# Gate weights in a pool of their own, their rows reused for the experts' outputs, and the last gate on VectorE alone

## The chip, the core and the metric

The kernel runs on one core of one Trainium2 chip. The metric is the device time of one execution in microseconds (us), as the median of several runs. Engines are called PE (TensorE, matrix products), DVE (VectorE), ACT (ScalarE), POOL (GpSimd) and SP (SyncE, which here only issues DMAs). "L794" is line 794 of the kernel before; in the changed kernel the numbers of the same lines are four or five less (L794 is L790 there, L815 is L811), and just above the edit one more (L505 is L506).

## What is computed

Three layers follow each other. Attention through a packed set of 32 queries per head gives a 512-wide row per token (4608 tokens). A dense layer pair with squared relu follows, and then a top-1 mixture of 8 experts:

```python
x = attn_out.transpose(0, 2, 1, 3).reshape(B * S, H * D)   # 4608 x 512
h = np.maximum(x @ w_in, 0.0)                              # 4608 x 2048
x = h * h @ w_out                                          # 4608 x 512
logits = x @ w_gate + modality_bias[modality_id]           # 4608 x 8
e_idx = np.argmax(logits, axis=1)
probs = softmax(logits); gate_w = probs[np.arange(N), e_idx]
for e in range(E):
    mask = e_idx == e
    h = np.maximum(x[mask] @ w1[e], 0.0)                   # 1024 wide
    out[mask] = gate_w[mask, None] * (h @ w2[e])
```

## The kernel before, in words

The dense pair works through the tokens in 12 units of 384 tokens (`NUN`, three tiles of 128 each, `UT`). For each of 16 pieces f of the hidden width, `layer1` makes `ph` in PSUM, relu and square on ACT, and splits the result into a rounded part and a remainder (`ghl`), so that three products of full-speed matmuls make one accurate product; `layer2` adds them into three banks `acc` (L492). At the end of a unit `evacuate` copies the three banks to the tile `row` in SBUF (two by ACT, L505; one by DVE, L503), and `tail` computes the gate: for each of the 3 token tiles and 8 experts one DVE instruction (L515) multiplies `row` by that expert's row of `wgb` and sums it into one logit. `wgb` holds the gate weights, copied to every partition: 8 rows of 512 numbers, 16 KB a partition. Then follow the bias, the softmax, a store of the rows to DRAM (`x2_d`), and `route`, which sorts the tokens into groups of 512 of one expert.

For every unit but the last the gate runs beside the next unit's matmuls. The last unit has nothing of the dense pair behind it. There the gate is shared out in the kernel before: experts 0 to 4 stay on DVE, and for experts 5 to 7 POOL makes the product into one tile `prod` (L519) and ACT sums it (L520): three tiles by three experts, nine pairs, which all use the one tile `prod`.

Behind that the experts start. `group(g)` takes 512 tokens of one expert: for each of eight pieces f it makes `h` in PSUM (L784), ACT writes the relu into the tile `ht` (L794), DVE writes its remainder (L795), and the second product (L806) adds into the banks `o`; DVE multiplies by the gate's probability (L815), and POOL scatters the row to `out` by an indirect DMA (L817). Weights come by DMAs that SP issues (`wraw`), and are split by ACT (L720) and DVE (L721) into `head`, `ring` and `wbt`. The first `h` of group 0 is already made while the last unit's second layer is running, since its tokens and weights are there.

SBUF room is handed on from stage to stage. `wgb` and `pp32` lie in the pool `pp`; with the pools `at` and `g` (which holds `ghl`, `r` and `prod`) it belongs to the stack `st3`. `st3` is closed behind the last gate, and the pools `o` (eight tiles for the experts' outputs, 16 KB a partition) and `h` (eight tiles `ht`) are opened over the same room:

```python
    other = [tail(NUN - 1), route(NTL - UT, NTL)]
    pull(other, 100)
    st3.close()
    held["o"] = ctx.enter_context(tc.tile_pool(name="o", bufs=8, side="left"))
    held["h"] = ctx.enter_context(tc.tile_pool(name="h", bufs=NFE, side="left"))
    tables(G_A, G_MAX)
    for g in range(G_ALL):
        with tc.high_priority(offset=200 if g == 0 else 0):
            group(g, g + 1 < G_ALL)
```

The order on each engine is made by a scheduler from the order of the code, priorities, and what waits for what. An instruction that writes the first tile of a pool waits for the last readers of the pools whose room it takes. Engines carry out their instructions in order.

Of the kernel before, what the change touches and what calls it, by code (L numbers as in the profile page):

```python
# [10 lines left out]
F32 = mybir.dt.float32  # L11
# [4 lines left out]
AF = mybir.ActivationFunctionType  # L16
ALU = mybir.AluOpType
# [3 lines left out]
P = 128  # L21
# [5 lines left out]
def tile_pack_attention_moe_moe2(  # L27
# [15 lines left out]
    nc = tc.nc  # L43
    B, H, D, S = kT_d.shape
    NPK = pT_d.shape[1] * 2 // (B * H)
    NT, DM = out.shape
    DFF = w_in64.shape[1]
    NE, _, FE = w1.shape
# [11 lines left out]
    NUN = NT // UW  # L60
# [5 lines left out]
    NTT = GT // P  # L66
# [15 lines left out]
    held = {"early": ps0.enter_context(tc.tile_pool(name="ps0", bufs=2, space=PSUM))}  # L82
    st1 = ExitStack()
    st2 = ExitStack()
    st3 = ExitStack()
    w_p = ctx.enter_context(tc.tile_pool(name="raw", bufs=2, side="left"))
    pp_p = st3.enter_context(tc.tile_pool(name="pp", bufs=1, side="left"))
    pw_p = st1.enter_context(tc.tile_pool(name="pw", bufs=1, side="right"))
    a_p = st2.enter_context(tc.tile_pool(name="a1", bufs=2, side="right"))
    
    ident = const.tile([P, P], F32, name="ident")
    make_identity(nc, ident)
    wgb = pp_p.tile([P, NE, DM], F32, name="wgb")
    pp32 = pp_p.tile([P, B, HP, 2 * NPK], F32, name="pp32")
    nc.gpsimd.memset(pp32, 0.0)
    pphl = pw_p.tile([P, PAIRS, 2, HP, 2 * P // 2], F32R, name="pphl")
# [38 lines left out]
    row = rows[:, : UT * XR].rearrange("p (t x) -> p t x", t=UT)  # L135
    junk = rows[:, UT * XR : UT * XR + DM]
# [118 lines left out]
    def bank(tag, name):  # L255
        if "early" in held:
            return held["early"].tile([P, 512], F32, tag="e", name=name, bufs=4)
        return held["all"].tile([P, 512], F32, tag=tag, name=name, bufs={"acc": 3, "h": 2, "t": 3}[tag])
# [128 lines left out]
    def second(f):  # L387
        return blocks(2 * f, 2).rearrange("p k x c f -> p (k x c f)").rearrange("p (x f) -> p x f", x=2)
# [118 lines left out]
    def tail(u):  # L507
        js = slice(u * UT, (u + 1) * UT)
        lg = lg_all[:, js, :]
        prod = held["g"].tile([P, DM], F32, tag="ghl", name="prod") if u == NUN - 1 else None  # L510
        for t in range(UT):
            for e in range(NE):
                one = lg[:, t, e : e + 1]
                if prod is None or e < 5:
                    nc.vector.scalar_tensor_tensor(  # L515
                        out=junk, in0=row[:, t, :DM], scalar=1.0, in1=wgb[:, e], op0=ALU.mult, op1=ALU.mult, accum_out=one
                    )
                else:
                    nc.gpsimd.tensor_tensor(out=prod, in0=row[:, t, :DM], in1=wgb[:, e], op=ALU.mult)  # L519
                    nc.scalar.activation(out=prod, in_=prod, func=AF.Copy, accum_out=one)  # L520
                if e % 2 == 1:
                    yield
        mx = mx_all[:, js]
        nc.vector.tensor_tensor(out=lg, in0=lg, in1=bias_all[:, js, :], op=ALU.add)
        nc.vector.tensor_reduce(out=mx, in_=lg, axis=AX.X, op=ALU.max)
        ex = x2_p.tile([P, UT, NE], F32, tag="ex", name="ex")
        sm = x2_p.tile([P, UT], F32, tag="sm", name="sm")
        nc.vector.tensor_tensor(out=ex, in0=lg, in1=mx.unsqueeze(2).to_broadcast([P, UT, NE]), op=ALU.subtract)
        nc.scalar.activation(out=ex, in_=ex, func=AF.Exp)
        nc.vector.tensor_reduce(out=sm, in_=ex, axis=AX.X, op=ALU.add)  # L530
        nc.vector.tensor_scalar(out=sm, in0=sm, scalar1=EPS, scalar2=None, op0=ALU.add)
        nc.vector.reciprocal(out=sm, in_=sm)
        nc.vector.tensor_copy(row[:, :, DM:XR], sm.unsqueeze(2).to_broadcast([P, UT, XR - DM]))
        nc.sync.dma_start(x2_d[u * UW : (u + 1) * UW].rearrange("(t p) x -> p t x", p=P), row)
        yield
# [187 lines left out]
    def weights1(g):  # L723
        er = nc.sync.value_load(ge_i[0:1, g : g + 1], min_val=0, max_val=NE - 1)
        for c in range(NDC):
            raw = w_p.tile([P, FE], F32, tag="raw", name="wraw")
            nc.sync.dma_start(raw, w1[bass.ds(er, 1), c * P : (c + 1) * P, :].rearrange("e p f -> p (e f)"))
            split_w(half1[:, g % 2, c], raw)
            yield

    def weights2(g):
        er = nc.sync.value_load(ge_i[0:1, g : g + 1], min_val=0, max_val=NE - 1)
        for i in range(0, NFE, 2):
            raw = w_p.tile([P, 2, DM], F32, tag="raw", name="wraw")
            nc.sync.dma_start(
                raw, w2[bass.ds(er, 1), i * P : (i + 2) * P, :].rearrange("e (c p) d -> p (e c) d", p=P)
            )
            for c in range(2):
                split_w(second(i + c), raw[:, c])
            yield  # L740
# [31 lines left out]
    def group(g, more):  # L772
        xs, gates = xts.pop(g)
        w2s = [weights2(g)]
        w1n, xn = ([weights1(g + 1)], [gathered(g + 1)]) if more else ([], [])
        hs = []
        for f in range(NFE):
            if f % 2 == 0:
                pull(w2s)
            ph = bank("h", "h3")  # L780
            i = 0
            for c in range(NDC):
                for x, y in ((0, 0), (0, 1), (1, 0)):
                    nc.tensor.matmul(  # L784
                        ph,
                        half1[:, g % 2, c, x, f * P : (f + 1) * P],
                        xs[c][:, y, :],
                        start=(i == 0),
                        stop=(i == 3 * NDC - 1),
                    )  # L790
                    i += 1
            h = held["h"].tile([P, 2, GT], F32R, tag="ht", name="ht")
            with tc.high_priority(offset=CHAIN):
                nc.scalar.activation(out=h[:, 0, :], in_=ph, func=AF.Relu)  # L794
                nc.vector.scalar_tensor_tensor(  # L795
                    out=h[:, 1, :], in0=ph, scalar=0.0, in1=h[:, 0, :].bitcast(F32), op0=ALU.max, op1=ALU.subtract
                )
            hs.append(h)
        pull(xn)
        for t in range(NTT):  # L800
            pull(w1n)
            po = bank("acc", "o3")
            i = 0
            for f in range(NFE):
                for x, y in ((0, 0), (0, 1), (1, 0)):
                    nc.tensor.matmul(  # L806
                        po,
                        hs[f][:, x, t * P : (t + 1) * P],
                        second(f)[:, y, :],
                        start=(i == 0),  # L810
                        stop=(i == 3 * NFE - 1),  # L811
                    )
                    i += 1
            o = held["o"].tile([P, DM], F32, tag="o", name="o")
            nc.vector.tensor_scalar(out=o, in0=po, scalar1=gates[t], scalar2=None, op0=ALU.mult)  # L815
            s = g * NTT + t
            put = nc.gpsimd.indirect_dma_start(  # L817
                out=out,
                out_offset=bass.IndirectOffsetOnAxis(ap=idx_s[:, s : s + 1], axis=0),
                in_=o,  # L820
                in_offset=None,
                bounds_check=NT - 1,
                oob_is_err=False,
            )
            if scattered:
                tc.declare_no_dep(put.ins, group="scatter", reason="each row of out belongs to one slot")
            tc.add_to_no_dep_group("scatter", put.ins)
            scattered.append(put)
            pull(xn, 2 if t == 1 else 1)

    def pull(gens, n=1):
        for _ in range(n):
            while gens:
                try:
                    next(gens[0])
                    break
                except StopIteration:
                    gens.pop(0)
# [95 lines left out]
    def background(u):  # L934
        gens, n = [], 0
        if u:
            gens, n = [tail(u - 1)], UT * NE // 2 + 1
        else:
            gens, n = [setup()], 1
        j1 = u * UT  # L940
        j0 = held.get("routed", 0)
        if j0 < J_A <= j1:
            gens += [route(j0, J_A), after_a()]
            n += 4 + J_A - j0 + 1 + NDC
            j0 = J_A
        if j1 > j0 and (j1 - j0 == NRT or j1 > J_A):
            gens.append(route(j0, j1))
            n += 4 + j1 - j0
            j0 = j1
        held["routed"] = j0  # L950
        return gens, n
# [40 lines left out]
    other = [tail(NUN - 1), route(NTL - UT, NTL)]  # L992
    pull(other, 100)
    st3.close()
    held["o"] = ctx.enter_context(tc.tile_pool(name="o", bufs=8, side="left"))
    held["h"] = ctx.enter_context(tc.tile_pool(name="h", bufs=NFE, side="left"))
    tables(G_A, G_MAX)

# [67 lines left out]
```

## Time and profile before

| | |
|---|---|
| time, median of 3 runs | 1307.05 us (1306.3 to 1307.85) |
| the profiled execution's own time | 1303.67 us |
| its span (first to last instruction) | 1301.9 us |
| PE busy | 1232.0 us, 95% of the span |
| DVE, ACT, POOL busy | 62%, 47%, 26% |
| mean granted clock of TensorE | 0.972 of full speed |

PE is busy for all but 70 us of the span. The page's chain of work that ended last goes over PE for 84% of the span. So what counts is when PE stands still and why. In the page's 40 slices of the span one slice of the second half stands out, with PE at 2 tenths: the one that holds the change from the dense pair to the experts, near 850 to 875 us. The page calls an engine's idle time by what ended it, which for a wait on several things is the one that came last.

### The profile page before, as it was taken

What the parts mean: (1) busy time and instruction counts of PE and PEld (TensorE: products, weight loads), DVE (VectorE), ACT (ScalarE), POOL (GpSimd) and SP (SyncE); (2) the same over time, 40 slices, a digit from 0 to 9 for tenths busy, and PEclk for the clock granted to TensorE, in tenths of its full rate; (3) what the DMA queues carried; (4) which work ended last, traced back from release to release, by engine and by line L of the source; (5) the groups of instructions that cost most, each with busy time, mean ns of one, the idle gap of its engine ahead of it and who ended that gap; (6) DMA issues with size and microseconds to landing.
All of it is one profiled execution on the core that took longest, in us unless ns stands there. A gap on an engine that the chain in (4) does not pass through costs nothing.

```text
span 1301.9 us, 18383 instructions
## 1 busy us (share of the span) xinstructions
PE 1232.0 (95%) x6356; PEld 1028.0 (79%) x6356; DVE 811.6 (62%) x2022; ACT 607.1 (47%) x1227; POOL 336.8 (26%) x398
## 2 busy tenths in 40 slices
PE   7899899999999999999999999929999999999995
PEld 4567777888888888888888888818788888888884
DVE  5886865849758694874867597875543444354341
ACT  3675565565555555455654556531433332343230
POOL 4663565322103231022310132040220221122011
PEclk8799999999999999999999999969999999999998
DMA  9876656332011221112121023320532542453210
GB/s 348 296 268 212 186 170 181 119 90 75 25 42 49 68 79 43 42 50 66 49 74 43 25 77 97 122 81 10 195 129 77 185 159 91 141 186 98 107 65 35
DMA packets 74167, 145.06 MB, mean 111 GB/s; under 512 B 6608, under 2 KB 26192, under 8 KB 73936
## 3 DMA queue, kind: packets, MB, share of 16 engines
q1 hardware_dynamic: 68304, 124.62, 29.9%
q0 software_dynamic: 5760, 19.17, 4.5%
q8 instruction: 52, 0.85, 0.3%
q14 instruction: 51, 0.42, 0.1%
HBM read 109.92 MB, written 33.85 MB: 110 GB/s over the span
## 4 chain that ended last, share of the span: by engine, by line
PE 84%; DVE 5%; DMA 4%; ACT 2%; POOL 2%; issue 2%; SPq 0%; POOLq 0%; ACTq 0%; DVEq 0%
PE acc L492 28%; PE ph L472 16%; PE h L784 15%; PE o L806 15%; PE pq L328 2%; PE s L427 2%; PE pw L360 2%; DMA wraw<-in_moe_w 2%; PE tr L764 1%; PE s L296 1%; POOL prod L519 1%; DMA wgb<-in_moe_w_out 1%; PE pq L329 1%; DMA rows<-in_moe_w_out 1%; PE ta L454 1%
## 5 line engine op out<-in xcount | busy, mean ns | idle before, releaser
L492 PE MATMUL acc<-wbt,ghl 128*128 128x512 f32 x1728 | 443.5, 399 | 0.0
L492 PEld LDWEIGHTS acc<-wbt,ghl 128*128 128x128 f32 x1728 | 315.9, 189 | 60.6 <-ACT ghl L483 0.4
L515 DVE SCALAR_TENSOR_TENSOR rows<-rows,wgb 128x512 f32<-128x512 f32 x279 | 218.9, 785 | 3.7
L784 PE MATMUL h<-xt,wbt 128*128 128x512 f32 x864 | 215.1, 399 | 0.7 <-DVE xt L768 0.4
L784 PEld LDWEIGHTS h<-xt,wbt 128*128 128x128 f32 x864 | 163.0, 189 | 40.3 <-DVE xt L768 0.7
L485 DVE TENSOR_TENSOR ghl<-r,ghl 128x384 fp32r<-128x384 f32 x176 | 108.0, 615 | 114.0 <-ACT ghl L483 113.2
L472 PE MATMUL ph<-a2T,ring 128*128 128x384 f32 (+1 forms) x840 | 145.7, 310 | 2.3 <-ACT ring L403 2.3
L483 ACT ACTIVATE ghl<-r 128x384 fp32r<-128x384 f32 x192 | 100.2, 522 | 97.5 <-PE acc L492 95.7
L472 PEld LDWEIGHTS ph<-a2T,ring 128*128 128x128 f32 x840 | 130.4, 191 | 10.6 <-ACT ring L403 2.8
L806 PE MATMUL o<-head,ht 128*128 128x512 f32 x432 | 113.9, 398 | 26.0 <-ACT ht L794 25.8
L481 ACT ACTIVATE r<-ph 128x384 f32<-128x384 f32 x192 | 92.9, 485 | 91.1 <-PE ph L472 85.1
L795 DVE SCALAR_TENSOR_TENSOR ht<-h,ht 128x512 fp32r<-128x512 f32 x72 | 49.3, 688 | 124.2 <-ACT ht L794 124.1
L472 PE MATMUL ph<-a2T,head 128*128 128x384 f32 (+1 forms) x696 | 119.4, 308 | 0.0
L806 PEld LDWEIGHTS o<-head,ht 128*128 128x128 f32 x432 | 81.2, 190 | 45.2 <-issue 26.2
L817 POOL DMA_INDIRECT out<-o,idx_s x36 | 36.7, 1018 | 299.3 <-DVE o L815 293.7
L806 PE MATMUL o<-ring,ht 128*128 128x512 f32 x432 | 112.2, 395 | 0.0
L794 ACT ACTIVATE ht<-h 128x512 fp32r<-128x512 f32 x72 | 42.5, 593 | 148.8 <-PE h L784 148.8
L472 PEld LDWEIGHTS ph<-a2T,head 128*128 128x128 f32 x696 | 106.5, 190 | 6.3
L482 ACT ACTIVATE r<-r 128x384 f32<-128x384 f32 x192 | 99.9, 522 | 4.1
L404 POOL TENSOR_TENSOR ring<-praw,ring 128x256 fp32r<-128x256 f32 x62 | 52.2, 843 | 168.8 <-ACT ring L403 123.6
L806 PEld LDWEIGHTS o<-ring,ht 128*128 128x128 f32 x432 | 80.3, 188 | 16.8
L721 DVE TENSOR_TENSOR wbt<-wraw,wbt 128x1024 fp32r<-128x1024 f32 x36 | 44.1, 1225 | 50.0 <-ACT wbt L720 49.8
(213 smaller groups left out, 1482.7 us busy)
## 6 DMA issues: line engine op xcount, KB each, us to landing
wraw<-in_moe_w SPq DMA_DIRECT2D x72, 512.0 KB, 3.7
praw<-pw_d SPq DMA_DIRECT2D x56, 256.0 KB, 3.9
pw_d<-pws SPq DMA_DIRECT2D x48, 256.0 KB, 3.1
x_d<-rows SPq DMA_DIRECT2D x12, 792.0 KB, 4.0
qT<-in_q SPq DMA_DIRECT2D x36, 256.0 KB, 3.7
early<-in_v SPq DMA_DIRECT2D x16, 512.0 KB, 6.6
rows<-in_k SPq DMA_DIRECT2D x10, 576.0 KB, 6.3
wgb<-in_moe_w_out SPq DMA_DIRECT2D x11, 512.0 KB, 4.5
```

The source lines that it names most:

```text
L404: nc.gpsimd.tensor_tensor(out=t[:, 1], in0=raw, in1=t[:, 0].bitcast(F32), op=ALU.subtract)
L472: nc.tensor.matmul(ph[:, off : off + n], t[:, x, c, :], a[:, y, c, off : off + n], start=(i == 0), stop=(i == 3 * NPC - 1),)
L481: nc.scalar.activation(out=r, in_=ph, func=AF.Relu)
L482: nc.scalar.activation(out=r, in_=r, func=AF.Square)
L483: nc.scalar.activation(out=hl[:, 0], in_=r, func=AF.Copy)
L485: eng.tensor_tensor(out=hl[:, 1], in0=r, in1=hl[:, 0].bitcast(F32), op=ALU.subtract)
L492: nc.tensor.matmul(acc[t], hl[:, x, t * P : (t + 1) * P], wbt[:, f, y, :], start=(f == 0 and x == 0 and y == 0), stop=(f == NF - 1 and x = ...
L515: nc.vector.scalar_tensor_tensor(out=junk, in0=row[:, t, :DM], scalar=1.0, in1=wgb[:, e], op0=ALU.mult, op1=ALU.mult, accum_out=one)
L721: nc.vector.tensor_tensor(out=t[:, 1, :], in0=raw, in1=t[:, 0, :].bitcast(F32), op=ALU.subtract)
L784: nc.tensor.matmul(ph, half1[:, g % 2, c, x, f * P : (f + 1) * P], xs[c][:, y, :], start=(i == 0), stop=(i == 3 * NDC - 1),)
L795: nc.vector.scalar_tensor_tensor(out=h[:, 1, :], in0=ph, scalar=0.0, in1=h[:, 0, :].bitcast(F32), op0=ALU.max, op1=ALU.subtract)
L806: nc.tensor.matmul(po, hs[f][:, x, t * P : (t + 1) * P], second(f)[:, y, :], start=(i == 0), stop=(i == 3 * NFE - 1),)
```

## The change

`wgb` gets a pool of its own, `wg`, which stays open to the end, below the pool `pp` in the same stack. The pool `o` is gone: the experts' outputs are written into the eight rows of `wgb` in turn. In the last unit's gate all 24 pieces run on DVE; `prod` is gone.

```diff
     w_p = ctx.enter_context(tc.tile_pool(name="raw", bufs=2, side="left"))
+    wg_p = ctx.enter_context(tc.tile_pool(name="wg", bufs=1, side="left"))
     pp_p = st3.enter_context(tc.tile_pool(name="pp", bufs=1, side="left"))
...
-    wgb = pp_p.tile([P, NE, DM], F32, name="wgb")
+    wgb = wg_p.tile([P, NE, DM], F32, name="wgb")
...
-        prod = held["g"].tile([P, DM], F32, tag="ghl", name="prod") if u == NUN - 1 else None
         for t in range(UT):
             for e in range(NE):
                 one = lg[:, t, e : e + 1]
-                if prod is None or e < 5:
-                    nc.vector.scalar_tensor_tensor(
-                        out=junk, in0=row[:, t, :DM], scalar=1.0, in1=wgb[:, e], op0=ALU.mult, op1=ALU.mult, accum_out=one
-                    )
-                else:
-                    nc.gpsimd.tensor_tensor(out=prod, in0=row[:, t, :DM], in1=wgb[:, e], op=ALU.mult)
-                    nc.scalar.activation(out=prod, in_=prod, func=AF.Copy, accum_out=one)
+                nc.vector.scalar_tensor_tensor(
+                    out=junk, in0=row[:, t, :DM], scalar=1.0, in1=wgb[:, e], op0=ALU.mult, op1=ALU.mult, accum_out=one
+                )
...
-            o = held["o"].tile([P, DM], F32, tag="o", name="o")
+            o = wgb[:, (g * NTT + t) % NE]
             nc.vector.tensor_scalar(out=o, in0=po, scalar1=gates[t], scalar2=None, op0=ALU.mult)
...
-    held["o"] = ctx.enter_context(tc.tile_pool(name="o", bufs=8, side="left"))
     held["h"] = ctx.enter_context(tc.tile_pool(name="h", bufs=NFE, side="left"))
```

The scheduler answers with another order from the end of the second layer to the first groups of experts; before that, and from group 3 on, the order is the same. On ACT, at the end of the last unit (`wbt` are weights of group 1, `rows<-acc` the copies of the banks), the kernel before has:

```order
L720 ACTIVATE wbt<-wraw 128x1024 x2
L505 ACTIVATE rows<-acc 128x512 x2
L720 ACTIVATE wbt<-wraw 128x1024
L520 ACTIVATE prod,lg_all<-prod 128x512 x9
L794 ACTIVATE ht<-h_8753 128x512
L794 ACTIVATE ht<-h_8769 128x512
```

and the changed kernel has, at the same place:

```order
L716 ACTIVATE wbt<-wraw 128x1024 x3
L506 ACTIVATE rows<-acc 128x512
L790 ACTIVATE ht<-h_8743 128x512
L790 ACTIVATE ht<-h_8759 128x512
L506 ACTIVATE rows<-acc 128x512
L790 ACTIVATE ht<-h_8781 128x512
```

The nine sums are gone, the first two `ht` of group 0 stand behind the first of the row copies, and the last piece of weights stands ahead of that copy, no longer behind both. On DVE, from the same moment on, the kernel before has:

```order
L721 TENSOR_TENSOR wbt<-wraw,wbt 128x1024
L515 SCALAR_TENSOR_TENSOR rows,lg_all<-rows,wgb 128x512 x2
L721 TENSOR_TENSOR wbt<-wraw,wbt 128x1024
L515 SCALAR_TENSOR_TENSOR rows,lg_all<-rows,wgb 128x512 x13
L524 TENSOR_TENSOR lg_all<-lg_all,bias_all 128x24
L525 TENSOR_REDUCE mx_all<-lg_all 128x3
L528 TENSOR_TENSOR ex<-lg_all,mx_all 128x24
L553 TENSOR_TENSOR s_8621<-lg_all,mx_all 128x24
L795 SCALAR_TENSOR_TENSOR ht<-h_8753,ht 128x512
```

and the changed kernel:

```order
L717 TENSOR_TENSOR wbt<-wraw,wbt 128x1024
L664 TENSOR_TENSOR lst<-pl,lst 128x92
L514 SCALAR_TENSOR_TENSOR rows,lg_all<-rows,wgb 128x512
L791 SCALAR_TENSOR_TENSOR ht<-h_8743,ht 128x512
L791 SCALAR_TENSOR_TENSOR ht<-h_8759,ht 128x512
L514 SCALAR_TENSOR_TENSOR rows,lg_all<-rows,wgb 128x512 x5
L791 SCALAR_TENSOR_TENSOR ht<-h_8781,ht 128x512
L514 SCALAR_TENSOR_TENSOR rows,lg_all<-rows,wgb 128x512 x5
L791 SCALAR_TENSOR_TENSOR ht<-h_8797,ht 128x512
```

The gate pieces (all 24 now) stand between the remainders of group 0, five between one and the next, and no longer ahead of them. On PE the three small routing matmuls (`pl`) stand behind the last nine of the second layer and no longer ahead of them:

```order
L493 MATMUL acc<-wbt,ghl 128x512 x15
L658 LDWEIGHTS om
L658 MATMUL pl<-od,om 128x184
...
L802 MATMUL o_8918<-head,ht 128x512 x2
L802 MATMUL o_8959<-head,ht 128x512 x2
L802 MATMUL o_9008<-head,ht 128x512 x2
L780 MATMUL h_8781<-xt,wbt 128x512 x12
```

This is the changed kernel; its first matmuls of the second expert product follow as before.

## Rows read from the trace of the kernel before

**Rows 1.** The page, busy time of each engine:
```profile
PE 1232.0 (95%) x6356; PEld 1028.0 (79%) x6356; DVE 811.6 (62%) x2022; ACT 607.1 (47%) x1227; POOL 336.8 (26%) x398
```

**Rows 2.** Waits of PE from 240 us on: total, times, longest (us):
```profile
PE o L806 <- ACT ht L794: 25.8, 1, 25.8
```

**Rows 3.** Timeline: start, length (us), engine, line, operation; where PE stops:
```profile
846.22 2.34 PE L492 MATMUL acc<-wbt,ghl 128*128 128x512 f32 x9
...
847.80 1.23 DVE L721 TENSOR_TENSOR wbt<-wraw,wbt 128x1024 fp32r<-128x1024 f32 x1 [1.39 <-ACT wbt L720]
...
849.36 1.06 ACT L720 ACTIVATE wbt<-wraw 128x1024 fp32r<-128x1024 f32 x1 [1.59 <-DMA wraw<-in_moe_w]
849.39 0.68 DVE L503 COPY rows<-acc 128x512 f32<-128x512 f32 x1
850.32 1.06 ACT L505 ACTIVATE rows<-acc 128x512 f32<-128x512 f32 x2
...
852.59 1.06 ACT L720 ACTIVATE wbt<-wraw 128x1024 fp32r<-128x1024 f32 x1 [1.21 <-DMA wraw<-in_moe_w]
```

**Rows 4.** The same timeline, inside the last unit's gate:
```profile
851.59 1.75 DVE L515 SCALAR_TENSOR_TENSOR rows<-rows,wgb 128x512 f32<-128x512 f32 x1
...
859.33 0.69 DVE L515 SCALAR_TENSOR_TENSOR rows<-rows,wgb 128x512 f32<-128x512 f32 x1
859.58 1.57 POOL L519 TENSOR_TENSOR prod<-rows,wgb 128x512 f32<-128x512 f32 x1 [0.83 <-ACT prod L520]
...
860.07 1.62 DVE L515 SCALAR_TENSOR_TENSOR rows<-rows,wgb 128x512 f32<-128x512 f32 x1
...
861.74 0.69 DVE L515 SCALAR_TENSOR_TENSOR rows<-rows,wgb 128x512 f32<-128x512 f32 x1
```

**Rows 5.** The same timeline, where PE goes on:
```profile
873.63 1.09 ACT L794 ACTIVATE ht<-h 128x512 fp32r<-128x512 f32 x2
...
874.33 2.90 PE L806 MATMUL o<-head,ht 128*128 128x512 f32 x6 [25.77 <-ACT ht L794]
874.33 0.69 DVE L795 SCALAR_TENSOR_TENSOR ht<-h,ht 128x512 fp32r<-128x512 f32 x1
```

**Rows 6.** Windows: stretch, its length, busy PE, PEld, DVE, ACT, POOL; clock; DMA:
```profile
852.50:854.50 2.00, 0.00 (x0) 0.00 (x0) 1.97 (x5) 1.67 (x3) 0.45 (x2) 0.59 0.70 242
854.50:874.00 19.50, 0.00 (x0) 0.00 (x0) 16.73 (x29) 6.15 (x17) 12.52 (x8) 0.50 0.09 29
...
878.00:880.00 2.00, 2.00 (x6) 1.53 (x5) 0.00 (x0) 0.00 (x0) 0.00 (x0) 0.50 0.79 298
880.00:882.00 2.00, 2.00 (x10) 1.62 (x9) 0.00 (x0) 0.55 (x1) 0.00 (x0) 0.96 0.00 0
```

**Rows 7.** Windows of the same kind, in the first stage:
```profile
30.00:32.00 2.00, 0.62 (x6) 0.48 (x5) 1.97 (x4) 0.63 (x1) 1.35 (x2) 1.00 1.02 363
32.00:34.00 2.00, 0.00 (x0) 0.00 (x0) 1.83 (x4) 1.02 (x2) 1.33 (x3) 0.91 1.01 392
```

**Rows 8.** Timeline of PE, start of group 1 and its pieces:
```profile
920.73 0.50 PE L784 MATMUL h<-xt,wbt 128*128 128x512 f32 x1 [0.23 <-ACT xt L767]
921.65 3.53 PE L784 MATMUL h<-xt,wbt 128*128 128x512 f32 x14 [0.42 <-DVE xt L768]
...
926.41 2.96 PE L784 MATMUL h<-xt,wbt 128*128 128x512 f32 x12
929.21 2.24 PE L806 MATMUL o<-head,ht 128*128 128x512 f32 x9
931.29 2.98 PE L784 MATMUL h<-xt,wbt 128*128 128x512 f32 x12
```

**Rows 9.** Windows, columns as in rows 6, of group 0:
```profile
873.60:916.60 43.00, 42.27 (x185) 34.22 (x186) 25.11 (x85) 9.00 (x16) 3.15 (x3) 0.92 0.10 37
916.60:921.60 5.00, 4.40 (x20) 3.01 (x18) 1.90 (x4) 2.27 (x5) 3.74 (x4) 1.00 0.99 334
```

**Rows 10.** Groups of DVE instructions, 280 to 835 us: count, busy us, mean ns:
```profile
L515 DVE SCALAR_TENSOR_TENSOR rows<-rows,wgb 128x512 f32<-128x512 f32 x240 | 181.2, 755 | 2.8
```

## The prediction, made before the result was known

> **What bounds the kernel now.** I read the busy times first: PE is busy 1232.0 us, 95% of the span [rows 1], so only its pauses are to be had. The list of PE's waits from 240 us on is next. One row holds nearly all of it: a single wait of 25.8 us, in front of the second expert product, put down to ACT's relu `ht` [rows 2]. The timeline around it shows where it lies. The last nine matmuls of the dense pair start at 846.22 and end at 848.56 [rows 3]; the first `o` starts at 874.33, 0.70 us after ACT began the first `ht` at 873.63 [rows 5]. The `h` that ACT reads there had long been made. What held `ht` back is the gate: on ACT it stands behind nine sums L520, and it takes room that `wgb` and `prod` held, so it waits for the last gate piece as well. The gate itself is a chain through the one tile `prod`: POOL's product takes 1.57 us, then ACT sums, then the next product; DVE starts a pair of its pieces in the same rhythm, 859.33 to 861.74, 2.41 us [rows 4]. Nine such rounds are 21.7 us, and the next thing on the chain is PE. So this stage is bound by the shared gate, with PE idle behind it.
>
> **What the change does, step by step.** It removes nine products on POOL and nine sums on ACT, with the 21.7 us chain. It adds nine gate pieces on DVE. And since `wgb` and `prod` no longer lie under the tiles `ht`, these wait only for the last uses of the dense pair's tiles, which are over at 848.56. That the first `ht` doesn't wait for the gate is seen in the order: the DVE remainder that needs it stands ahead of 23 of the 24 gate pieces.
>
> *When PE starts again.* ACT's order decides. The last piece of weights now stands ahead of the row copies. Its data were there at 852.59 [rows 3]; what sets that time (the DMA, which follows when DVE has split the second piece, 847.80 + 1.23) stands in the same order as before, so I keep it. Then 1.06 us for that piece, 0.53 for one row copy (two take 1.06) [rows 3]: 854.18. The first `ht` starts there, and PE 0.70 us later [rows 5]: 854.88. The other need of the first `o` is the DVE copy of row 1. DVE has six small routing pieces and the third split ahead of it. From the end of the second split at 849.03, the split (1.23) starts when ACT is through with it, at 849.36 + 1.06 = 850.42, and the copy takes 0.68 [rows 3]: done by 852.4, hidden. The three routing matmuls, moved behind the second layer, run in PE's pause. So the pause is 848.56 to 854.88, 6.3 us where it was 25.8, and **19.5 us are gained**.
>
> *Whether DVE keeps up.* Gate pieces now stand between the remainders of group 0, so PE waits for DVE if five pieces and one remainder last longer than PE's step. A piece starts 0.74 us after the one before when POOL is still (859.33 to 860.07) [rows 4]; 5 x 0.74 + 0.69 (one remainder [rows 5]) = 4.4 us. PE's step is twelve `h` (926.41 to 929.21, 2.80) and some nine `o` (to 931.29, 2.08): 4.9 us [rows 8]. Over the whole group: DVE's other work between the gate and the start of group 1 was 25.1 + 1.9 = 27.0 us [rows 9]; 24 pieces are 17.8; 44.8 in all. PE takes 874.33 to 921.65, 47.3 us, for that stretch [rows 5, 8]. It fits, with 2.5 us to spare. I cost it at nothing; PE's matmuls are the cover. The bounds of that zero: in the kernel before, group 1 began with small pauses of 0.23 and 0.42 us [rows 8], which may go, and the order now puts more routing pieces ahead of the last `xt` and the first remainder of group 1, which I allow 3 us, a little more than the spare 2.5.
>
> The Trainium skill speaks against this step in "Perfetto Trace Analysis", section Optimizing Scalar/DVE Operations: if DVE is saturated, handing work to Scalar or GpSimd may make sense, and here DVE was busy 16.73 of 19.50 us of the pause [rows 6]. The same section adds that handing work between GpSimd and DVE might not help, since they share an SBUF read port. The trace sides with the second half: beside a product on POOL a piece takes 1.62 us, without one 0.69 [rows 4], and 240 pieces of the other units take 0.755 on average [rows 10]. By the first half the pieces would stay as long as now, which is the third case below; by the second they take 0.74, as in the sum.
>
> *The clock.* PE's clock was still partly up in 852.5 to 854.5 (0.59) and at half after that; it came back between 878 and 882 (0.50, then 0.96: at about 880.2) [rows 6]. So 874.33 to 880.2 ran at half clock, which cost about 2.9 us. Now the pause is a quarter as long. Either the clock falls all the same and the 2.9 us are paid again (nothing changes), or it stays up and they are gained too. In the first stage six short matmuls at 30 to 32 us and none at 32 to 34 were enough to let it fall (0.91 in the second of these windows) [rows 7], and the new pause, with three tiny matmuls in it, looks like that. I take the fall.
>
> *The rest costs nothing.* Evicting into rows of `wgb` keeps eight buffers in turn and the same waits for the scatters; the first of them stands behind all 24 gate pieces on the same engine, so it finds `wgb` free. POOL loses work it did while idle otherwise. The store of the last unit's rows, its routing and SP's loads of later groups' numbers move by a few us; only groups 7 and up need them, six groups later. On SP two loads of weights now stand ahead of those number loads; both wait for room freed by PE's last use of `head`, as before.
>
> **The sum.** The profiled execution took 1303.67; 19.5 less is 1284.2. The three runs shown lie higher, median 1307.05, by 3.4 us, so I forecast 1307.05 - 19.5 = **1287.5 us**.
>
> **The rivals.**
> - *The forecast*: 62%. Its own range is 1286 to 1289.
> - *The clock stays up* in the shorter pause: 2.9 us more, 1284.6. For it: the pause is a quarter as long. Against it: rows 7. 20%.
> - *Gate pieces stay slow*, at the mean of the pairs now, 2.41 / 2 = 1.2 us. Then DVE needs 24 x 1.2 + 27.0 = 55.9 us for the 47.3 of PE, 8.6 are lost again: 1296. For it: half the pieces in the gate take 1.62 and the first one 1.75 [rows 4]. Against it: rows 10. 6%.
> - *A new pause at the start of group 1*: routing pieces, table pieces and the last `xt` collide on DVE, 3 us: 1290.5. 6%.
> - *No change*, because `ht` still waits for something that ends with the gate, which the order speaks against, or because pieces take 1.66 us, at which DVE's 66.8 us eat the whole gain: 1307. 4%.
> - *Slower*, the other side: every piece takes as long as the first in the gate now, 1.75 + 0.08 for reading the sum, 1.83. DVE needs 43.9 + 27.0 = 70.9 us in group 0, PE waits 23.6 in its steps, 4.1 more than is gained: 1311. It decides from 1.66 us a piece on, and shows as slower by 0.2% from 1.77. Against it: in the gate now, pieces without a product on POOL beside them take 0.69. 2%.
>
> **How the numbers follow.** The likeliest case gives 1287.5. The range 1283 to 1292 reaches down to the clock that stays up (1284.6, less the 1.5 us of its own spread) and up to the new pause at group 1 (1290.5 and 1.5); it leaves out 12%. A difference of 0.2% (2.6 us) is about what a measurement of this kernel can tell from no change. Faster: 62 + 20 + 6 + 6 = 94%; same 4%; slower 2%.
>
> **What would show it.** PE's longest wait near 850 us is about 6 us and is put down to `ht` behind a row copy or the weights' DMA, no longer to a chain through `prod`. No L519 or L520 is left. The 24 pieces lie 0.74 us apart, in fives, with a remainder behind each five, and PE has no idle time before an `h` of group 0. Group 1 starts about 47 us after the first `o`. From there on every step is as long as before, and the whole is shifted. I am wrong if DVE's pieces are long without POOL, if PE pauses in each step of group 0, if the first `ht` waits for weights that come later than 852.6, or if later groups show waits for the scatters out of `wgb`.

## The result, and the profile after

| | median us | runs | ratio to before, 95% |
|---|---|---|---|
| before | 1306.67 | 1305.84 to 1307.85 (4) | |
| changed | 1284.63 | 1282.85 to 1288.47 (4) | 0.9835 [0.9808, 0.9861] |

The change gains 22.0 us, 1.65%. The profiled execution of the changed kernel took 1283.14 us (span 1281.3), that of before 1303.67 (1301.9): 20.6 us between the spans.

The list of PE's waits from 240 us on answers [rows 2]:

```profile
PE o L802 <- ACT ht L790: 3.2, 1, 3.2
PE o L802 <- DVE wgb L811: 0.2, 1, 0.2
```

The wait for `ht` is 3.2 us where it was 25.8, and both pauses at the start of group 1 [rows 8] are gone. The timeline at the place where PE stops and goes on (start, length, engine, line, operation) answers [rows 3, 5]:

```profile
847.54 3.65 PE L493 MATMUL acc<-wbt,ghl 128*128 128x512 f32 x15
850.09 1.06 ACT L716 ACTIVATE wbt<-wraw 128x1024 fp32r<-128x1024 f32 x1 [2.32 <-DMA wraw<-in_moe_w]
...
852.55 1.06 ACT L716 ACTIVATE wbt<-wraw 128x1024 fp32r<-128x1024 f32 x1 [1.40 <-DMA wraw<-in_moe_w]
853.52 0.58 ACT L506 ACTIVATE rows<-acc 128x512 f32<-128x512 f32 x1
853.99 1.08 ACT L790 ACTIVATE ht<-h 128x512 fp32r<-128x512 f32 x2
854.63 2.93 PE L802 MATMUL o<-head,ht 128*128 128x512 f32 x6 [3.19 <-ACT ht L790]
...
857.36 4.47 PE L780 MATMUL h<-xt,wbt 128*128 128x512 f32 x12
861.67 2.23 PE L802 MATMUL o<-head,ht 128*128 128x512 f32 x9
```

The second layer ends at 847.54 + 3.65 = 851.19 and the first `o` starts at 854.63: the pause is 3.4 us (before: 25.8). The chain into it is the one predicted: data of the fourth weight piece, its rounding on ACT, one row copy, the first `ht`, PE. The first gate piece on DVE starts only at 854.95, so `ht` no longer waits for the gate.

The same timeline on DVE inside the gate (the second and third of five pieces, and the next two remainders) answers [rows 4]:

```profile
857.48 0.69 DVE L514 SCALAR_TENSOR_TENSOR rows<-rows,wgb 128x512 f32<-128x512 f32 x1
858.22 0.69 DVE L514 SCALAR_TENSOR_TENSOR rows<-rows,wgb 128x512 f32<-128x512 f32 x1
...
862.50 0.69 DVE L791 SCALAR_TENSOR_TENSOR ht<-h,ht 128x512 fp32r<-128x512 f32 x1 [2.11 <-ACT ht L790]
...
867.38 0.69 DVE L791 SCALAR_TENSOR_TENSOR ht<-h,ht 128x512 fp32r<-128x512 f32 x1 [0.65 <-ACT ht L790]
```

Pieces start 0.74 us apart, and DVE, not PE, is the one that waits at each remainder. The windows (columns as in [rows 6]) show the clock:

```profile
852.00:854.00 2.00, 0.00 (x0) 0.00 (x0) 1.53 (x4) 1.45 (x3) 0.00 (x0) 0.96 0.16 35
854.00:856.00 2.00, 1.37 (x3) 1.16 (x4) 2.00 (x5) 1.56 (x4) 0.00 (x0) 0.50 0.76 235
...
858.00:860.00 2.00, 2.00 (x6) 1.52 (x6) 1.90 (x7) 0.00 (x0) 0.00 (x0) 0.50 0.04 10
860.00:862.00 2.00, 2.00 (x9) 1.62 (x8) 0.38 (x2) 0.13 (x1) 0.00 (x0) 0.83 0.00 0
862.00:864.00 2.00, 2.00 (x11) 1.62 (x10) 1.47 (x4) 0.47 (x1) 0.00 (x0) 1.00 0.00 0
```

It fell in the short pause too, and six `o` and most of twelve `h` ran at half clock, 1.2 GHz: 854.63 to 861.67, 7.0 us.

**Where the 20.6 us lie.** Times of two traces can only be subtracted from a common mark. One of the routing matmuls late in the dense pair, on PE's timeline of before and of after:

```profile
823.50 0.25 PE L662 MATMUL pl<-od,om 128*128 128x184 f16 x1
```

```profile
826.41 0.25 PE L658 MATMUL pl<-od,om 128*128 128x184 f16 x1
```

This execution was already 2.9 us behind there. Up to that mark both kernels have the same order of work, so I count the 2.9 us as spread between runs and not as an effect of the change; that is argued, not shown (the last section returns to it). Behind the mark, the pause gives 25.77 - 3.44 = 22.3 and the two pauses at group 1 give 0.65: 22.3 + 0.65 - 2.9 = 20.05 of the 20.6. The other half microsecond is not placed.

### The profile page after: what moved, and what is told of

Its sections match the earlier page's. It is cut to its first block, busy times and chain, and to the rows that moved or that the text cites. A ratio compares the mean times of both kernels' runs of the same rounds, so it can differ in the third digit from the quotient of the medians.

```text
span 1281.3 us, 18377 instructions
## 1 busy us (share of the span) xinstructions
PE 1234.5 (96%) x6356; PEld 1029.2 (80%) x6356; DVE 810.7 (63%) x2040; ACT 600.7 (47%) x1209; POOL 323.9 (25%) x389
## 4 chain that ended last, share of the span: by engine, by line
PE 86%; DVE 5%; DMA 5%; ACT 2%; issue 1%; POOL 1%; SPq 0%; POOLq 0%; ACTq 0%; DVEq 0%
PE acc L493 28%; PE ph L473 16%; PE h L780 15%; PE o L802 15%; PE s L428 2%; PE pq L329 2%; PE pw L361 2%; DMA wraw<-in_moe_w 1%; PE tr L760 1%; PE s L297 1%; DMA wgb<-in_moe_w_out 1%; DMA rows<-in_moe_w_out 1%; PE pq L330 1%; PE ta L455 1%; PE ta L320 1%
## 5 line engine op out<-in xcount | busy, mean ns | idle before, releaser
L813 POOL DMA_INDIRECT out<-wgb,idx_s x36 | 36.5, 1013 | 342.5 <-DVE wgb L811 251.4
```

## The experiments

**One: the gate on VectorE alone, pools as before.** The nine products and sums become DVE pieces; `wgb` stays in `pp` and `o` in its own pool.

```diff
-        prod = held["g"].tile([P, DM], F32, tag="ghl", name="prod") if u == NUN - 1 else None
...
-                if prod is None or e < 5:
-                    nc.vector.scalar_tensor_tensor(...)
-                else:
-                    nc.gpsimd.tensor_tensor(out=prod, in0=row[:, t, :DM], in1=wgb[:, e], op=ALU.mult)
-                    nc.scalar.activation(out=prod, in_=prod, func=AF.Copy, accum_out=one)
+                nc.vector.scalar_tensor_tensor(...)
```

> The kernel before, with all 24 last gate pieces on VectorE and no products on POOL or sums on ACT; the gate weights stay in the pool that gives its room to the tiles ht. Theory (room decides): ht still waits for the last reader of wgb. 24 pieces 0.74 us apart are 17.8 us behind the third split on DVE, so the gate ends near 871 where it ended at 873.6; PE's pause is 22 to 24 us and the time is 2 to 4 us under the kernel before, about 1303 to 1305. Rival (the gate on VectorE alone is what gains): the pause is about 6 us as in the changed kernel and the time about 1285.

**Two: the pools alone.** The changed kernel, with the shared gate and its `prod` in the pool `g` put back.

```diff
+        prod = held["g"].tile([P, DM], F32, tag="ghl", name="prod") if u == NUN - 1 else None
...
+                    nc.gpsimd.tensor_tensor(out=prod, in0=row[:, t, :DM], in1=wgb[:, e], op=ALU.mult)
+                    nc.scalar.activation(out=prod, in_=prod, func=AF.Copy, accum_out=one)
```

> The changed kernel's pool for the gate weights and its rows for the experts' outputs, but the last gate shared with POOL and ACT through prod as in the kernel before; prod lies in a pool that gives its room to the tiles ht. Theory (room decides): prod alone holds ht back until its last sum, the chain of nine rounds at 2.41 us is as before, PE's pause is 24 to 26 us and the time within 2 us of the kernel before, 1305 to 1308. Rival (a pool of its own for the gate weights is enough): the pause is about 6 us and the time about 1285.

**Three: the pools, and the shared gate with its products elsewhere.** The products go to a part of `rows` that is free at that time, which gives room to no `ht`; the output of DVE's pieces, which nobody reads, goes to a PSUM bank.

```diff
+        prod = junk if u == NUN - 1 else None
+        thrown = bank("t", "thrown") if u == NUN - 1 else junk
...
+                        out=thrown, in0=row[:, t, :DM], scalar=1.0, in1=wgb[:, e], op0=ALU.mult, op1=ALU.mult, accum_out=one
```

> As the pool-only kernel, but the products go to the unused part of the tile rows, whose room no ht takes, and VectorE's thrown-away output to a PSUM bank; the gate stays shared with POOL and ACT. Theory (room decides, who does the gate doesn't): ht starts behind the row copies and PE's pause is 6 to 8 us. ACT's nine sums stand between ht pieces and DVE's fifteen pieces fit PE's steps even at 1.7 us in pairs (15 x 1.2 = 18, as the 24 x 0.74 = 17.8 of the changed kernel), so the time is within 3 us of the changed kernel, 1283 to 1288. Rival (VectorE alone is needed as well): the chain through prod, 2.41 us a round, holds up ACT and with it ht in group 0, five or more pauses of 1 to 3 us, 1292 or more.

| | median us | before in that group | ratio, 95% |
|---|---|---|---|
| one: VectorE alone | 1305.97 | 1308.05 | 0.9983 [0.9955, 1.0012] |
| two: pools alone | 1306.68 | 1308.05 | 1.0003 [0.9989, 1.0018] |
| three: pools, products elsewhere | 1284.85 | 1308.05 | 0.9833 [0.9813, 0.9852] |

PE's waits from 240 us on, of the first, then of the second, then of the third:

```profile
PE o L801 <- ACT ht L789: 23.4, 2, 23.1
```

```profile
PE o L807 <- DVE ex L529: 25.3, 1, 25.3
```

```profile
PE o L808 <- ACT ht L796: 2.7, 1, 2.7
PE h L786 <- DVE ht L797: 0.7, 2, 0.4
PE h L786 <- DVE xt L770: 0.6, 1, 0.6
```

Room decides, in all three. In the first, all 24 pieces run without a break, 860.46 to 878.08, and `ht` still starts behind the last of them. ACT, with no sums left to do, stands idle for 18.11 us until then:

```profile
878.20 1.09 ACT L789 ACTIVATE ht<-h 128x512 fp32r<-128x512 f32 x2 [18.11 <-DVE rows L513]
```

The pause is 2.7 us shorter than before, the time 2.1 by the medians, as the theory had it, and not to be told from nothing by the interval. In the second, `prod` alone holds the pause. (The release is put down to DVE's `ex`; ACT's last sum ends just ahead of it, at 877.65, and the first `ht` starts at 877.67.) That the nine sums stand ahead of `ht` on ACT follows from the room as well: in the third, with the same nine sums on ACT, the first two `ht` start at 854.32 and the first sum at 856.98. Only with both tiles away does the pause go, and then it goes with the shared gate too, which leaves 1.3 us in three small waits of `h`. So the edit to the gate gains nothing by what it takes off POOL and ACT; it gains by removing `prod` from that pool. DVE's pieces in the third experiment and in the changed kernel, grouped by form (count, busy us, mean ns, idle before):

```profile
L517 DVE SCALAR_TENSOR_TENSOR thrown<-rows,wgb 128x512 f32<-128x512 f32 x15 | 17.8, 1186 | 0.3
```

```profile
L514 DVE SCALAR_TENSOR_TENSOR rows<-rows,wgb 128x512 f32<-128x512 f32 x24 | 16.5, 689 | 0.6
```

Fifteen pieces beside POOL cost DVE more (17.8 us) than 24 alone (16.5). The shared gate took no load off DVE at all. (It is not the PSUM bank: in experiment two, with the output in `rows` as in the changed kernel, fifteen took 18.1 us.) The Trainium skill, "Perfetto Trace Analysis", section Optimizing Scalar/DVE Operations, says that moving work between GpSimd and DVE may not help because they share an SBUF read port. The two rows agree with the outcome; no run here shows the port.

**Four: each gate piece twice. Five: four times.** The changed kernel, with the last unit's pieces repeated (`range(4 ...)` in the fifth).

```diff
-                nc.vector.scalar_tensor_tensor(
+                for _ in range(2 if u == NUN - 1 else 1):
+                    nc.vector.scalar_tensor_tensor(
```

> The changed kernel with each of the 24 last gate pieces done twice (the second writes the same values again): 17.8 us more of VectorE in group 0. Theory (the prediction's sum of VectorE): 2.5 us are spare in group 0, the rest is lost, 17.8 - 2.5 = 15 us, between 1297 and 1301, as pauses of PE in front of o or h in each step of group 0. Rival (there is more slack, since pieces slip behind the remainders and into groups 1 and 2): less than 8 us lost, under 1293.

Twice: 1283.41 us, ratio 0.982 [0.9804, 0.9837]: nothing lost against the changed kernel's 1284.63 (0.9835), so the theory fell. PE waits 2.5 us for the first `ht` and 0.2 later. The windows show where the work went, first of the changed kernel, then of this one (its first stage ended some 7 us later, so its groups lie that much further right):

```profile
900.00:946.00 46.00, 46.00 (x210) 37.24 (x209) 25.73 (x48) 15.04 (x23) 8.58 (x12) 1.00 0.38 136
```

```profile
900.00:946.00 46.00, 46.00 (x215) 37.27 (x214) 39.13 (x113) 15.16 (x25) 10.10 (x13) 1.00 0.47 155
```

The last repeated piece starts at 920.58, well in group 1, and routing pieces follow it; PE stays busy for 46.00 of 46.00 us. Is there an end to it?

> The changed kernel with each of the 24 last gate pieces done four times (the same values written again): 53 us more of VectorE. With each done twice nothing was lost. Theory (pieces slide behind the remainders of later groups, in each of which DVE is idle some 25 of 46 us, and what needs the gate is due only in group 7): within 3 us of the changed kernel. Rival (DVE is full from group 0 to group 2 and PE waits for ht, xt or the outputs): 10 us or more lost.

Four times: 1303.87 us, 0.997 [0.9957, 0.9984]. Most of the gain is lost, so this theory fell too: 15.3 us by the median of the changed kernel run in the same group (1288.58, below), 19.5 us by the traces, from the mark used above (827.43 here) to the end of the span. PE's waits name the place:

```profile
PE o L803 <- DVE wgb L812: 19.0, 2, 18.7
PE o L803 <- ACT ht L791: 1.7, 1, 1.7
```

And its DVE timeline there:

```profile
913.72 0.69 DVE L515 SCALAR_TENSOR_TENSOR rows<-rows,wgb 128x512 f32<-128x512 f32 x1
914.46 0.69 DVE L515 SCALAR_TENSOR_TENSOR rows<-rows,wgb 128x512 f32<-128x512 f32 x1
915.08 0.75 DVE L812 TENSOR_SCALAR wgb<-o,gt 128x512 f32<-128x512 f32 x1
```

From 892 to 915 us DVE does nothing but gate pieces, and group 0's first output, which takes the row of expert 0 in `wgb`, stands behind the pieces that read that row. PE needs that output's bank for group 1 and stands still. This is the new wait that the changed pool brings: a row of `wgb` can take an output only when its gate pieces are through. Of the 96 pieces 69 stand ahead of that output, the last reader of the row of expert 0 (the third token tile's) among them; in the changed kernel that reader is the 17th of 24. So 51 of the 72 added pieces bear on this wait, 51 x 0.74 = 38 us. With 18.7 us lost there (and 1.3 in two waits for `xt`), the spare before it bites is about 38 - 20 = 18 us, an estimate from this one profile. In the changed kernel the 17th piece ends at 873.3, the last at 879.2, and the first such output starts at 890.23.

**Six: the copies ahead of the weights.** What is left of the pause is ACT's queue. The third and fourth weight piece of group 1 now stand behind the row copies (`held` keeps the copies' instructions) on ACT and DVE.

```diff
+            if g == 1 and c >= 2:
+                with tc.issue_after(held["copied_s"].ins), tc.issue_after(held["copied_v"].ins):
+                    split_w(half1[:, g % 2, c], raw)
+            else:
                 split_w(half1[:, g % 2, c], raw)
```

> The changed kernel, with the third and fourth weight piece of group 1 (not needed for another 45 us) queued on ACT and DVE behind the copies of the last rows, so that the first ht stands behind one copy alone. Theory (what is left of the pause is ACT's queue: weight pieces that wait for their DMA stand ahead of the copies): first o 0.55 (copy) + 0.7 = 1.3 us behind PE's last matmul, where it is 3.4; 2 us less, and up to 3 more if the clock stays up: 1279.5 to 1283, 2 to 5 under the changed kernel. Rival (something else sets the first ht, or the clock falls whatever the length): pause stays above 3 us or no gain, 1283.5 to 1288.

**Seven: the pause filled.** Twelve matmuls that nobody reads, behind the second layer's last (`held["last2"]`).

```diff
+    fill = bank("t", "fill")
+    with tc.high_priority(offset=1000), tc.issue_after(held["last2"].ins):
+        for _ in range(12):
+            nc.tensor.matmul(fill, half1[:, 0, 0, 0, :P], xts[0][0][0][:, 0, :], start=True, stop=True)
```

> The changed kernel with twelve more matmuls (128x512, into a bank that nobody reads) on PE between the last of the second layer and the first expert product, 12 x 0.233 = 2.8 us of the 3.2 us in which PE waited. Theory (the clock falls because PE stands still there): the granted clock stays at 1.00, the first six o take about 1.5 us where they took 2.9 and the next twelve h 3.0 where they took 4.5, so it is 2.9 us faster, 1280 to 1283. Rival (the price of the clock is made up elsewhere, or the clock falls all the same): within 1 us of the changed kernel. The pause itself is as long as before, 3 to 3.6 us, part of it now filled.

Beside them, **the changed kernel once more**:

> The changed kernel once more, unaltered, beside the runs of this group: 1283 to 1288, PE's wait for the first ht near 3.2 us, the clock at half for some 7 us.

| | median us | runs | ratio to before (1308.93), 95% |
|---|---|---|---|
| changed, again | 1288.58 | 1283.89 to 1290.9 (5) | 0.9835 [0.9813, 0.9857] |
| six: copies first | 1280.62 | 1278.32 to 1285.08 (5) | 0.9789 [0.9765, 0.9814] |
| seven: filled | 1283.72 | 1280.39 to 1284.34 (5) | 0.9806 [0.9786, 0.9825] |

The timeline of ACT and PE with the copies first:

```profile
849.24 3.65 PE L493 MATMUL acc<-wbt,ghl 128*128 128x512 f32 x15
852.46 0.60 ACT L506 ACTIVATE rows<-acc 128x512 f32<-128x512 f32 x1 [2.98 <-PE acc L493]
...
852.98 1.09 ACT L794 ACTIVATE ht<-h 128x512 fp32r<-128x512 f32 x2
853.63 1.71 PE L806 MATMUL o<-head,ht 128*128 128x512 f32 x6 [0.48 <-ACT ht L794]
...
855.17 2.98 PE L784 MATMUL h<-xt,wbt 128*128 128x512 f32 x12
857.99 2.24 PE L806 MATMUL o<-head,ht 128*128 128x512 f32 x9
```

The timeline of PE with the pause filled:

```profile
854.24 3.05 PE L991 MATMUL fill<-xt,wbt 128*128 128x512 f32 x12
857.13 0.33 PE L658 MATMUL pl<-od,om 128*128 128x184 f16 x2
857.93 1.70 PE L802 MATMUL o<-head,ht 128*128 128x512 f32 x6 [0.46 <-ACT ht L790]
859.46 3.05 PE L780 MATMUL h<-xt,wbt 128*128 128x512 f32 x12
862.36 1.32 PE L802 MATMUL o<-head,ht 128*128 128x512 f32 x5
```

In both the granted clock is 1.00 in every window of 2 us from 848 to 876. Filled, the six `o` and twelve `h` take 857.93 to 862.36, 4.4 us where the changed kernel took 7.0: the fall cost 2.6 us there, and standing still is what brings it on. In the second profile of the changed kernel, taken beside these, the clock fell later and the same 18 matmuls took 6.0 us (863.54 to 869.56), a price of 1.6. With the copies first the pause is 852.89 to 853.63, 0.7 us, and from the end of the second layer to the second round of `o` it is 5.1 us where the changed kernel took 10.5 (851.19 to 861.67): 2.7 from the pause, 2.7 from the clock. Some of that is lost again: two later waits for `ht` take 0.5 and 0.6 us. From the mark (828.11 with the copies first, 829.58 filled) to the end of the span it is 451.1 and 452.4 us, where the two profiles of the changed kernel have 454.9 and 454.2. So by the traces the copies gain 3 to 4 us and the filling some 2. The medians differ by more (8.0 and 4.9 us from the changed kernel beside them), but the changed kernel's five runs spread over 7 us; the intervals of the filled kernel and the changed one overlap, those of the sixth and the changed one just touch. The filled kernel's median lies 0.7 us above the range of its theory, and the changed kernel's 0.6 above its own. The rows, of one profile each, carry these two verdicts; the medians agree in sign. The sixth is the fastest kernel here, 28 us under the kernel before beside it.

## Why the prediction was right, and where it was not

*The bound.* Right. The 25.8 us were room, and one and two against three show that it was the room of `wgb` and of `prod`, each enough by itself to keep the pause.

*When PE starts again.* The mechanism was right, the term was mis-sized: 6.3 us forecast, 3.4 measured, 2.9 too small a gain. The step that failed reads "what sets that time (the DMA, which follows when DVE has split the second piece) stands in the same order as before, so I keep it". The piece's data came at 852.55, almost the forecast 852.59, but PE's stop was at 851.19, not 848.56: behind PE's stop it came 1.4 us, where before it was 4.0. From the data on, the chain took 2.1 us for a forecast 2.3. What moved lies further up on DVE, ahead of the rows shown with the change. These are the remainders of the last second-layer weights of group 0, first before, then changed:

```profile
838.70 0.69 DVE L721 TENSOR_TENSOR ring<-wraw,ring 128x512 fp32r<-128x512 f32 x1 [0.95 <-ACT ring L720]
839.44 0.68 DVE L721 TENSOR_TENSOR ring<-wraw,ring 128x512 fp32r<-128x512 f32 x1
842.53 0.69 DVE L721 TENSOR_TENSOR head<-wraw,head 128x512 fp32r<-128x512 f32 x1
```

```profile
839.71 0.68 DVE L717 TENSOR_TENSOR head<-wraw,head 128x512 fp32r<-128x512 f32 x1
840.92 0.69 DVE L717 TENSOR_TENSOR ring<-wraw,ring 128x512 fp32r<-128x512 f32 x1 [0.53 <-ACT ring L716]
841.60 0.69 DVE L717 TENSOR_TENSOR ring<-wraw,ring 128x512 fp32r<-128x512 f32 x1
```

The `head` remainder, which stood behind both `ring` remainders and ten routing pieces, now stands ahead of them. It frees one of the two buffers `wraw`, so the four weight pieces of group 1, which take turns in them, start earlier. On PE the last four `ph` matmuls, which read the old `head`, moved ahead of an expert product. The profile of experiment one has `head` early as well (its fourth piece comes 2.5 us behind PE's stop, less than the 4.0 of before and more than the 1.4 here), that of experiment two has it late (3.7). That this order gave the 2.7 us is read from these rows and was not tried by itself; that the weights' place on ACT sets the length of the pause was tried, by experiment six.

*Whether DVE keeps up.* The zero was right, its reckoning was not. I held all of DVE's 27.0 us of other work in that stretch to be due before group 1 and found 2.5 us spare. Twice the gate, 17.8 us more, cost nothing, and four times showed some 18 us spare ahead of the first output. Some 12 of the 27.0 are neither remainders nor outputs, weights or `xt`: most of it is routing that PE needs six groups later, and with the gate done twice some of it ran in group 1. The 3 us allowed for a new pause at group 1 went the other way: the two small pauses there are gone, 0.65 us.

*How long a piece is.* Right: 0.74 us apart, mean 689 ns; the rivals with 1.2 and 1.83 us needed POOL beside them. Rows 4 are read a little too simply, though: the piece of 0.69 us overlaps a product as well (859.58 to 860.02). It had started first; the slow piece starts while the product runs and ends 0.54 us after it (861.69 and 861.15).

*The clock.* It fell again, as forecast, at a price of 2.6 us in the first profile and 1.6 in the second (forecast 2.9). The measured 1284.63 is by chance the number of the rival "the clock stays up": that rival's 2.9 us came from the earlier weights instead. The clock rows tell the two apart, the time can't.

*The rest.* The scatters out of `wgb` cost no wait, as forecast. But "it finds `wgb` free" rests on the same spare: experiment five is what it costs once that cover is gone.

*The sum.* 19.5 forecast, 22.0 measured [18.2 to 25.1, from the ratio's interval]: 19.5 + 2.9 (the pause) + 0.65 (group 1) = 23.05, which is 1.0 above the difference of the medians and within its interval.

## What to carry to other kernels

A tile that gives its room to the next stage holds that stage up until its last reader is through, whatever engine that is; look for every tile in the room, since removing one of two gained nothing here. To find an end of slack on an off-path engine, double its work instead of adding up what it does between two marks: work that is due later slides. When an edit makes a scheduler place code anew, compare the order of everything that the next transfer's buffer waits for, not of the edited lines only.

## What the runs showed of the hardware

Nearly the whole difference between two runs of one program lay in its start. The changed kernel was profiled twice; these are the windows of the first 100 us, first of the run shown above, then of the one beside experiments six and seven:

```profile
0.00:100.00 100.00, 80.96 (x437) 56.50 (x437) 71.88 (x176) 57.24 (x116) 57.73 (x86) 0.83 0.86 298
```

```profile
0.00:100.00 100.00, 82.70 (x415) 58.12 (x415) 68.87 (x170) 50.18 (x104) 51.19 (x81) 0.74 0.87 293
```

The second had a lower granted clock there (0.74 for 0.83) and finished fewer instructions on every engine. The first `ph` of the dense pair starts at 145.02 in it and at 136.92 in the first, 8.1 us later; the routing matmul used as a mark above starts at 834.90, 8.5 us later; and its span is 7.8 us longer (1289.1). That the clock is the cause is not shown: the profile of before has 0.83 in this window, as the first one here, and its first `ph` still starts 2.4 us earlier (134.49). Times of places in two traces should be taken from such a mark.

A short stop need not cost the clock. It stayed at 1.00 through stops of 0.5 us (copies first, filled) and of 1.7 us (gate four times, first `ht`). It went to 0.50 with those of 2.5 us (gate twice), 2.7 us (products elsewhere), 3.4 us (changed kernel) and 3.9 us (its second profile), but not always within the stop. In the second profile of the changed kernel PE stood still from 859.68 to 863.54, but for three routing matmuls, and the clock was at 1.00 to the end of that; it fell with PE at work again, near 865, and was back near 868.4:

```profile
862.00:864.00 2.00, 0.46 (x2) 0.42 (x3) 1.61 (x4) 2.00 (x5) 0.00 (x0) 1.00 0.54 206
864.00:866.00 2.00, 2.00 (x8) 1.26 (x7) 2.00 (x5) 0.46 (x1) 0.00 (x0) 0.75 0.59 159
...
868.00:870.00 2.00, 2.00 (x9) 1.61 (x8) 1.25 (x4) 0.24 (x1) 0.00 (x0) 0.89 0.00 0
```

So what a stop costs has to be read from the clock behind it too, and it differs between two runs of one program.
